# RWKV attention and a mixing MLP in one kernel: five hand-ordered engine queues replaced by a list scheduler's order

## The chip, the cores and the metric

The kernel runs on one core of one Trainium2 chip. Time is device microseconds of one execution, from the launch of the program to its end. Three runs of the kernel before took 586.89, 587.65 and 588.23 us, so the median is 587.65 us.

## The reference, cut to what matters

```python
# attention: 4 batches, 8 heads, 768 steps, head width 48, all fp32
for t in range(S):
    cur = einsum('bhd,bhe->bhde', u * k_t, v_t)
    y[:, :, t] = einsum('bhd,bhde->bhe', r_t, state + cur)
    state = w * state + einsum('bhd,bhe->bhde', k_t, v_t)
# the heads side by side are x [4, 768, 384]; then, for each batch
h = x.transpose(0, 2, 1) @ U @ V               # mixes the 768 steps, rank 32
u = x + h.transpose(0, 2, 1)
out = u + max(u @ w_ch1, 0) @ w_ch2            # 384 -> 1536 -> 384
```

The four weights `U`, `V`, `w_ch1` and `w_ch2` arrive as float64. The kernel reads them as pairs of 32-bit words and builds the fp32 value with integer operations.

## The kernel before, in words

**Attention.** The sequence of a batch is cut into 6 chunks of 128 steps, each of two halves of 64. Powers of `w` in tables (`tabT`, `tab`, `tabr`) turn the decay inside a chunk into plain products. Chunk n goes through preparation, two parts and an end.
- *Preparation.* `a_tr_r` and `a_tr_k` (lines 381 to 389) turn r and k so that the head width lies on the partitions, and scale them by `tabT`. Batch 0 does the turn with TensorE; batches 1 to 3 load r and k a second time as blocks of 32 by 32 (`a_load_blocks`, line 303, 32 DMAs for three chunks) and turn them on VectorE (line 369), with the product on GpSimd (line 371). `a_ks` (line 324) and `a_dv` (lines 331 to 334) are products on GpSimd; `a_dg` is a sum on VectorE, followed by 8 small multiplications on ScalarE (line 345), or in batch 0 by one product on VectorE (line 342).
- *Parts.* `a_part(n, 0)` and `a_part(n, 1)` issue some 60 small matmuls each: the output of chunk n and, between them, the scores and the state update of chunk n + 1. VectorE then masks the scores (`am`, line 557) and adds the state (`S`, line 581). The decayed state is made right behind that sum: one product on VectorE in batch 0 (line 583), four small multiplications on ScalarE in the others (line 585). The next part needs it.
- *End.* `a_x` (line 566) writes x. When all six chunks of a batch are there, `c_g` and `c_u` (lines 591 to 615) do the rank-32 mix. For batches 1 to 3 u is stored to HBM (`c_store`, line 669), read back as blocks (`c_blocks`, line 677) and turned on VectorE (`c_turn`, lines 689 to 691).

**MLP.** Each batch is two blocks of 384 steps with 12 hidden slices of 128. `m_1` makes one slice with 9 matmuls of 128x128 by 128x384, ScalarE its rounded high part `hh` (line 708), VectorE the remainder `hl` (line 709), and `m_2` (line 713) adds the slice to three outputs, again with 9 matmuls: 432 in a batch. `m_1` of the next slice stands between the two. The last slice adds u (line 726) and stores the output (line 728). The w_ch1 and w_ch2 matrices come as 24 units: DMA (line 174), conversion on ScalarE and VectorE (lines 182 to 191), the high half on ScalarE (line 201), the low half on GpSimd (line 202).

**Order.** Batch 0's attention is the front, and no MLP can run beside it. The attention of batch b + 1 is spread over the MLP of batch b at positions written by hand (`attn_slots`, line 753: loads at t0 - 9, preparation and parts at fixed steps). TensorE and SyncE, the engine that issues nearly all DMAs, follow that written order from the first MLP on; VectorE, ScalarE and GpSimd follow it from the MLP of batch 1 on, and before that an order that the framework works out. Each engine takes its queue strictly in turn, so an instruction whose data is not there holds all behind it. `wake` (line 76) adds matmuls without use to the front.

Of the kernel before, what the change touches and what calls it, by code (L numbers as in the profile page):

```python
# [19 lines left out]
W_HI = 1.0  # L20


@with_exitstack
def rwkv_moe(ctx: ExitStack, tc: tile.TileContext, r, k, v, w, u, U, V, w1, w2, out):
# [21 lines left out]
    NVS = 3  # L46
# [4 lines left out]
    ps = ctx.enter_context(tc.tile_pool(name="ps", bufs=1, space=bass.MemoryType.PSUM))  # L51

    def ps_tile(tag, name, bufs):
        return ps.tile([128, 512], F32, tag=tag, name=name, bufs=bufs)
# [5 lines left out]
    ident = const.tile([128, 128], F32, name="ident")  # L60
    make_identity(nc, ident)
    mask = const.tile([128, C2], F32, name="mask")
    nc.gpsimd.memset(mask, 1.0)
    for g in range(2):
        nc.gpsimd.affine_select(out=mask[g * C2:(g + 1) * C2], in_=mask[g * C2:(g + 1) * C2], pattern=[[1, C2]],
                                compare_op=ALU.is_gt, fill=0.0, base=0, channel_multiplier=-1)
# [7 lines left out]
    nc.scalar.copy(first_act, ident[0:1, 0:1])  # L74

    def wake(n):

        pt = ps_tile("mm", "p_wake", 2)
        for _ in range(n):
            nc.tensor.matmul(pt[:, :128], lhsT=ident, rhs=ident, start=True, stop=True)  # L80

    wT = const.tile([PD, NP, 1], F32, name="wT")
    nc.sync.dma_start(wT[:HP, :, 0], bass.AP(tensor=w.tensor, offset=w.offset, ap=[[1, HP], [2 * D, NP]]))
    nc.sync.dma_start(wT[HP:, :, 0], bass.AP(tensor=w.tensor, offset=w.offset + D, ap=[[1, D], [2 * D, NP]]))
    ub = const.tile([128, H, D], F32, name="ub")

    def tables():

        HC = C2 // 2
        NS = HC.bit_length()  # L90
        wc = const.tile([PD, NP, 1], F32, name="wc")
        nc.vector.tensor_scalar(wc, wT, W_LO, W_HI, ALU.max, ALU.min)
        sq = const.tile([PD, 2, NP, NS], F32, name="sq")
        pw = work.tile([PD, 2, NP, HC], F32, name="pw", tag="am", bufs=4)
        nc.gpsimd.memset(pw[:, :, :, 0:1], 1.0)
        nc.vector.tensor_copy(sq[:, 0, :, 0:1], wc)
        for i in range(1, NS):
            nc.vector.tensor_mul(sq[:, 0, :, i:i + 1], sq[:, 0, :, i - 1:i], sq[:, 0, :, i - 1:i])
        nc.vector.reciprocal(sq[:, 1], sq[:, 0])
        for i in range(NS - 1):  # L100
            m = 2 ** i
            for x_ in range(2):
                nc.vector.tensor_mul(pw[:, x_, :, m:2 * m], pw[:, x_, :, 0:m],
                                     sq[:, x_, :, i:i + 1].broadcast_to([PD, NP, m]))
        top = [sq[:, x_, :, NS - 1:] for x_ in range(2)]
        nc.vector.tensor_mul(tabT[:, 0, :, :HC], pw[:, 0], top[1].broadcast_to([PD, NP, HC]))
        nc.scalar.copy(tabT[:, 0, :, HC:C2], pw[:, 0])
        nc.vector.tensor_mul(tabT[:, 1, :, :HC - 1], pw[:, 1, :, 0:HC - 1],
                             pw[:, 0, :, HC - 1:].broadcast_to([PD, NP, HC - 1]))
        nc.scalar.copy(tabT[:, 1, :, HC - 1:2 * HC - 1], pw[:, 1])  # L110
        nc.gpsimd.tensor_copy(tabT[:, 1, :, C2 - 1:C2], top[1])
        for x_ in range(2):
            nc.scalar.copy(tabT[:, x_, :, C2:], tabT[:, x_, :, :C2])
        for x_, t in ((1, tab), (0, tabr)):
            pt = ps_tile("tr", f"pt_tab{x_}", 1)
            for q in range(NP):
                nc.tensor.transpose(pt[:, q * PE_:q * PE_ + PD], tabT[:, x_, q, :], ident[:PD, :PD])
            nc.scalar.copy(t.rearrange("p (h d) -> p h d", d=D), pt.rearrange("p (h d) -> p h d", d=HP)[:, :, :D])
        nc.vector.tensor_mul(wm, top[0], top[0])

    def flags():

        wrow = work.tile([1, DM], F32, name="wrow", tag="xh", bufs=NXS)
        nc.sync.dma_start(wrow, w.rearrange("(o h) d -> o (h d)", o=1))
        wrc = work.tile([1, DM], F32, name="wrc", tag="xh", bufs=NXS)
        nc.vector.tensor_scalar(wrc, wrow, W_LO, W_HI, ALU.max, ALU.min)
        nc.vector.tensor_tensor(wrc, wrc, wrow, ALU.not_equal)
        outside = const.tile([1, 1], F32, name="outside")
        nc.vector.tensor_reduce(outside, wrc, AX.X, ALU.max)
        nc.vector.tensor_copy(flag, outside)  # L130

    flag = const.tile([1, 1], I32, name="flag")
    tabT = const.tile([PD, 2, NP, C], F32, name="tabT")
    wm = const.tile([PD, NP, 1], F32, name="wm")
    tab = const.tile([128, DM], F32, name="tab")
    tabr = work.tile([128, DM], F32, name="tabr", tag="xl", bufs=NXS)
# [3 lines left out]

    NBIG = 30
# [4 lines left out]
    def big(shape, dt, name):  # L146
        return xpool.tile(shape, dt, tag="big", name=name, bufs=NBIG)

    Uf = const.tile([128, NCH, R], F32, name="Uf")
    V3 = const.tile([3 * R, S], F32R, name="V3")  # L150
# [6 lines left out]
    turn = [False]  # L157

    def unit(name, shape, parts, split):

        P_ = shape[0]
        n = 1
        for s_ in shape[1:]:
            n *= s_
        got = []

        def view(ap, two=1):
            return ap if len(shape) == 2 else ap.rearrange("p (a c) -> p a c", a=shape[1])

        def load():  # L170
            t = big([128, 2 * n], I32, f"raw_{name}") if wide else big([128, n], F32, f"raw_{name}")
            got.append(t[:P_])
            for p0, ap in parts:
                nc.sync.dma_start(view(t[p0:p0 + ap.shape[0]]), ap.bitcast(I32) if wide else ap)

        def convert():
            v_ = got.pop()
            if wide:
                word = v_.rearrange("p (n two) -> p two n", two=2)
                low, high = word[:, 0], word[:, 1]  # L180
                byte = v_.bitcast(U8).rearrange("p (n e) -> p n e", e=8)[:, :, 3]
                nc.scalar.activation(high.bitcast(F32), high.bitcast(F32), AF.Copy, scale=2.0 ** -112)
                if turn[0]:

                    nc.scalar.activation(low.bitcast(F32), byte, AF.Relu, scale=-2.0 ** -5, bias=c_top[:P_])
                    nc.scalar.activation(low, low.bitcast(F32), AF.Copy, scale=-1.0, bias=C_TOP)
                else:
                    nc.vector.tensor_scalar(low, byte, 2.0 ** -5, 7.0, ALU.mult, ALU.min)
                turn[0] = not turn[0]
                nc.vector.scalar_tensor_tensor(low, high, 3, low, ALU.logical_shift_left, ALU.bitwise_or)  # L190
                nc.vector.scalar_tensor_tensor(low, high, -2 ** 31, low, ALU.bitwise_and, ALU.bitwise_or)
                v_ = low.bitcast(F32)
            split(view(v_))
        return load, convert

    def weight_units():
        units = []

        def split(hi, lo):
            def go(sv):  # L200
                nc.scalar.copy(hi, sv)  # L201
                nc.gpsimd.tensor_tensor(lo, sv, f32(hi), ALU.subtract)
            return go

        def split_to(d, key, name):
            def go(sv):
                t = big([128, 2, DM], F32R, name)
                d[key] = t
                split(t[:, 0], t[:, 1])(sv)
            return go  # L210

        def u_split(sv):
            nc.scalar.copy(Uf, sv)

        def v_split(sl):
            def go(sv):
                nc.scalar.copy(V3[:, sl], sv)
                nc.vector.tensor_tensor(V3[2 * R:, sl], sv[2 * R:], f32(V3[2 * R:, sl]), ALU.subtract)
            return go

        units.append(unit("u", [128, NCH, R], [(0, U.rearrange("(c p) r -> p c r", p=128))], u_split))
        for j in range(S // DM):
            sl = slice(j * DM, (j + 1) * DM)
            units.append(unit(f"v_{j}", [3 * R, DM], [(i * R, V[:, sl]) for i in range(3)], v_split(sl)))
# [12 lines left out]
    loaded = {}  # L237
    wide_r = {}
    wide_k = {}
    pre = {}  # L240
    trs = {}
    scs = {}
    xs = {}
    St = {}


    def on_dve(n):
        return n >= NCH

    def a_load(n):  # L250
        b, c = divmod(n, NCH)
        ts = []
        if n < 4:
            t3 = xpool.tile([128, 2 * H * HP + DM], F32, tag="uTl" if n % 2 else "uTh", name=f"ld_{n}", bufs=2)
            rk = t3[:, :2 * H * HP].rearrange("p (i h d) -> p i h d", i=2, h=H)
            ts = [rk[:, 0], rk[:, 1], t3[:, 2 * H * HP:].rearrange("p (h d) -> p h d", h=H)]
            for i, (t, src) in enumerate(zip(ts, (r, k, v))):
                q = nc.scalar if n < 3 and i == 1 else nc.sync
# [282 lines left out]
    def a_done(n, row):  # L541
# [4 lines left out]
        if row == 0:  # L546
            return
# [440 lines left out]
```

## Time and profile before

| | |
|---|---|
| median of three runs | 587.65 us |
| profiled execution, its own time | 588.04 us |
| its span, first to last instruction | 586.2 us |
| TensorE matmul busy | 450.8 us (77%), 5023 matmuls |
| VectorE busy | 241.6 us (41%) |
| ScalarE busy | 180.5 us (31%) |
| GpSimd busy | 173.5 us (30%) |
| mean granted TensorE clock | 0.856 of full speed |

One execution is profiled. Busy time of an engine is the time in which at least one of its instructions runs; idle time counts against the kernel only where that engine, or one that waits for it, sets the end. The granted clock is given as a share of 2.4 GHz: 1.00 is that level and 0.50 is 1.2 GHz. SPq is the instruction queue of SyncE.

### The profile page before, as it was taken

The page shows a single profiled execution, that of the slowest core. Times are in us where ns is not written, and L with a number is a line of the kernel's source. Part 1 is how long each engine was busy: PE and PEld are TensorE (multiplying, and loading weights), DVE is VectorE, ACT ScalarE, POOL GpSimd, SP SyncE. Part 2 cuts the span into 40 slices and gives each one's busy share as a digit, 9 for nine tenths or more (in the row PEclk, how much of TensorE's full clock was granted, in tenths as well). Part 3 has the DMA queues.
Part 4 walks back from the last instruction along what each step waited for, and adds up shares of the span by engine and source line. Part 5 has one row for each costly group of instructions (what it writes and reads, how often), then busy time and mean ns, then how long its engine had stood idle before and what let it go on. Part 6 is the DMA issues. An engine that isn't in the chain of part 4 may idle for free.

```text
span 586.2 us, 12398 instructions
## 1 busy us (share of the span) xinstructions
PE 450.8 (77%) x5023; PEld 417.9 (71%) x5023; DVE 241.6 (41%) x516; ACT 180.5 (31%) x536; POOL 173.5 (30%) x168
## 2 busy tenths in 40 slices
PE   6647778356869996718958999707949999899994
PEld 6546668245758995718857998707948899799994
DVE  6657438948652424122425424213414523322211
ACT  2351127355542521105414422104324522221110
POOL 4633204756435101025433301007505500220000
PEclk8567659759888998859979999858898999999998
DMA  9999002972266005965563004866265102600101
GB/s 153 180 316 349 4 13 62 136 115 33 49 121 97 3 1 135 159 97 91 79 103 82 6 3 104 168 97 110 49 85 92 43 2 60 142 2 1 40 1 45
DMA packets 210833, 50.23 MB, mean 86 GB/s; under 512 B 201617, under 2 KB 207506, under 8 KB 210770
## 3 DMA queue, kind: packets, MB, share of 16 engines
q1 hardware_dynamic: 206018, 48.50, 42.4%
q10 hardware_dynamic: 4752, 0.89, 1.1%
q8 instruction: 41, 0.67, 0.5%
q14 instruction: 22, 0.18, 0.1%
HBM read 40.50 MB, written 8.85 MB: 84 GB/s over the span
## 4 chain that ended last, share of the span: by engine, by line
PE 33%; SPq 15%; DVE 4%; DMA 4%; POOL 4%; ACT 3%; issue 3%; DVEq 0%; POOLq 0%; ACTq 0%
PE p L480 27%; SPq L303 10%; SPq L677 2%; PE pav L434 2%; DMA ub<-ud 2%; ACT dv L345 2%; PE pav L440 1%; SPq L285 1%; DMA ud<-x 1%; SPq L273 1%; POOL rT L371 1%; POOL dv L331 1%; DMA bl<-in_r_dram 1%; DVE x L726 1%; DVE x L615 1%
## 5 line engine op out<-in xcount | busy, mean ns | idle before, releaser
L480 PE MATMUL p<-uTh,w1s 128*128 128x384 f32 x570 | 171.9, 356 | 27.8 <-ACT w1s L201 16.1
L480 PE MATMUL p<-w2s,hh 128*128 128x384 f32 x564 | 152.0, 349 | 0.0
L480 PE MATMUL p<-w2s,hl 128*128 128x384 f32 x288 | 101.0, 351 | 47.9 <-DVE hl L709 47.9
L480 PEld LDWEIGHTS p<-uTh,w1s 128*128 128x128 f32 x570 | 110.8, 200 | 34.6 <-ACT w1s L201 17.0
L709 DVE SCALAR_TENSOR_TENSOR hl<-p,hh 128x384 fp32r<-128x384 f32 x96 | 53.0, 553 | 174.9 <-ACT hh L708 174.8
L480 PEld LDWEIGHTS p<-w2s,hh 128*128 128x128 f32 x564 | 106.8, 198 | 1.1
L480 PE MATMUL p<-uTl,w1s 128*128 128x384 f32 x288 | 102.5, 356 | 3.8 <-POOL uTl L691 3.8
L708 ACT ACTIVATE hh<-p 128x384 fp32r<-128x384 f32 x96 | 46.8, 487 | 151.2 <-PE p L480 150.9
L480 PEld LDWEIGHTS p<-w2s,hl 128*128 128x128 f32 x288 | 57.0, 198 | 49.5 <-DVE hl L709 49.5
L480 PEld LDWEIGHTS p<-uTl,w1s 128*128 128x128 f32 x288 | 57.7, 200 | 7.4 <-POOL uTl L691 6.7
L691 POOL TENSOR_TENSOR uTl<-ut,uTh 128x384 fp32r<-128x384 f32 x21 | 21.7, 1033 | 134.0 <-ACT uTh L690 133.9
L345 ACT ACTIVATE dv<-ldv,dg 128x48 f32<-128x48 f32 x144 | 34.3, 322 | 74.3 <-DVE dg L340 69.8
L400 PE MATMUL pab<-rT,kT 48*64 48x64 f32 x768 | 35.6, 246 | 23.2 <-DVE S L581 16.5
L371 POOL TENSOR_TENSOR kT<-kT,tabT 112x512 f32<-112x512 f32 x18 | 23.2, 1296 | 94.5 <-DVE kT L369 90.3
L400 PEld LDWEIGHTS pab<-rT,kT 48*64 48x64 f32 x768 | 29.1, 154 | 25.4 <-issue 16.0
L585 ACT ACTIVATE S<-S,wm 112x48 f32<-112x48 f32 x120 | 30.3, 323 | 51.3 <-DVE S L581 51.2
L434 PE MATMUL pav<-vsw,am 64*64 64x48 f32 x384 | 37.4, 246 | 2.7 <-ACT seen L503 2.7
L440 PE MATMUL pav<-S,rT 48*64 48x48 f32 x704 | 37.7, 239 | 0.0
L434 PEld LDWEIGHTS pav<-vsw,am 64*64 64x64 f32 x384 | 31.0, 157 | 7.6 <-ACT seen L503 4.2
L440 PEld LDWEIGHTS pav<-S,rT 48*64 48x64 f32 x704 | 33.7, 157 | 0.2 <-issue 0.2
L434 PE MATMUL pav<-ldv,am 64*64 64x48 f32 x320 | 30.8, 239 | 3.9 <-DVE x L566 2.8
L371 POOL TENSOR_TENSOR rT<-rT,tabT 112x512 f32<-112x512 f32 x18 | 23.4, 1306 | 32.7 <-DVE rT L369 32.7
(122 smaller groups left out, 582.7 us busy)
## 6 DMA issues: line engine op xcount, KB each, us to landing
raw_w<-in_moe_w_ch_dram SPq DMA_DIRECT2D x24, 384.0 KB, 7.9
out_dram<-x SPq DMA_DIRECT2D x24, 192.0 KB, 2.4
bl<-in_k_dram SPq DMA_DIRECT2D x95, 48.0 KB, 2.5
bl<-in_r_dram SPq DMA_DIRECT2D x95, 48.0 KB, 2.4
ud<-x SPq DMA_DIRECT2D x21, 192.0 KB, 2.0
ub<-ud SPq DMA_DIRECT2D x84, 48.0 KB, 2.3
ldr<-in_r_dram SPq DMA_DIRECT2D x20, 192.0 KB, 3.6
ldk<-in_k_dram SPq DMA_DIRECT2D x20, 192.0 KB, 4.1
```

Of the source, the lines that this page charges most:

```text
L303: nc.sync.dma_start(t[32 * g:32 * g + 32, q, :, :ln], sv)
L345: nc.scalar.activation(dv[:, h], vt[:, h], AF.Copy, scale=dg[:, h:h + 1])
L371: nc.gpsimd.tensor_mul(xT[:PD], xT[:PD], tabT[:, i])
L400: return [lambda q=q, i=i: nc.tensor.matmul(pt[(i ^ j) * C2:(i ^ j) * C2 + C2, q * C2:(q + 1) * C2], lhsT=kT[rows, q, i * C2:(i + 1) * C2] ...
L434: return nc.tensor.matmul(to(q, j, i), lhsT=am[j][half, q, :], rhs=vsw[n][half, q, :] if j else vt[half, 2 * q, :], start=(row == 0 and q ...
L440: return nc.tensor.matmul(to(q, row, i), lhsT=rT[rows, q, i * C2:(i + 1) * C2], rhs=St[n, i][rows, q, :], start=False, stop=(row == 1 and ...
L480: last_mm[:] = [nc.tensor.matmul(*args, **kw)]
L585: nc.scalar.activation(sn[:, q], sn[:, q], AF.Copy, scale=wm[:, q])
L677: nc.sync.dma_start(bt[32 * g:32 * g + 32], rows[:, :, c0:c0 + 32])
L691: nc.gpsimd.tensor_tensor(ul[:, ct, :], ut, f32(uh[:, ct, :]), ALU.subtract)
L708: i_hh = nc.scalar.activation(hh, pt, AF.Relu)
L709: i_hl = nc.vector.scalar_tensor_tensor(hl, pt, 0.0, f32(hh), ALU.max, ALU.subtract)
```

## The change

All work of the fast path is first recorded as operations, each with its engine, a duration in ns, the buffers that it reads and writes, and a key. `Plan.schedule` then plays all five engines forward: of the operations that are ready it takes the one that can start first (at equal starts the one with the smaller key), moves that engine's clock on, lets DMAs land after a modelled time, and gives buffers of a ring out in their order of use. The instructions of all five engines are issued in the order of the starts that this gives, from the first one on. The steps written by hand become keys only.

```diff
+    AFTER = {"DVE": 33, "ACT": 33, "PE": 54, "POOL": 79, "SP": 28}
+    ISSUE = 42
+    LANDS = 1650
+    ...
+                now = min(t for t, _, _ in at)
+                for t, o, i in sorted((a for a in at if a[0] <= now + 1), key=lambda a: a[1].key):
+                    done = t + o.ways[i][1]
+                    if any(j != i and max(free[w[0]], self.ready_on(o, w[0]), lock if w[3] else 0) + w[1] < done - 1
+                           for j, w in enumerate(o.ways)):
+                        continue
+    ...
+    def run(self):
+        self.schedule()
+        for o in sorted(self.ops, key=lambda o: (o.start, o.n)):
+            o.fn()
+def dve(n):
+    return 130 + 1.09 * n
+def act(n):
+    return 285 + 0.6 * n
+def pool(n):
+    return 180 + 2.15 * n
```

Operations marked with `lock` are never planned at the same time on VectorE and GpSimd. Two-operand steps with both operands in SBUF get two ways, and the scheduler takes the one that ends first; this covers `a_ks`, both products of `a_dv`, the product with `tabT`, the low halves of the weights and of u, and the decayed state. The multiplication by `dg` may go to ScalarE (8 small ones) or to VectorE (one), and one step of the weight conversion to VectorE or ScalarE.

```diff
+    def on_either(n, fn, w_, r_, dk=0.0):
+        return op("POOL", pool(n), lambda: fn(nc.gpsimd), w_, r_, lock=True, dk=dk,
+                  alt=[("DVE", dve(n), lambda: fn(nc.vector), True)])
```

The state is kept undecayed. The sum that the chain waits for is one VectorE operation whose second operand was multiplied by the decay earlier, beside the matmuls; the table `tab` is scaled to match, and `tabr` and its two products in batch 0 are gone.

```diff
-                nc.vector.tensor_tensor(sn, ptv, St[n, i], ALU.add)
-                if plain(n):
-                    nc.vector.tensor_mul(sn, sn, wm.broadcast_to([PD, NP, D]))
-                for q in range(0 if plain(n) else NP):
-                    nc.scalar.activation(sn[:, q], sn[:, q], AF.Copy, scale=wm[:, q])
+                on_dve(192, lambda e, new=new, ptv=ptv, dec=decayed[n, j]: e.tensor_tensor(new.t, ptv(), dec.t, ALU.add),
+                       [new], [pt, decayed[n, j]])
+            dec = decayed[nk] = wbuf([PD, NP, D], F32, "SW", 2, f"SW_{nk[0]}_{nk[1]}")
+            on_either(192, lambda e, dec=dec, new=new: e.tensor_mul(dec.t, new.t, wm.t.broadcast_to([PD, NP, D])),
+                      [dec], [new, wm])
```

`m_2` issues the six matmuls with `hh` first and the three with `hl` last. All `wake` calls are gone. The blocks of r and k get a ring of 5 buffers of their own, and the pool that they shared with the weights goes from 30 to 25.

```diff
-            whole(pt, lhsT=hh[:, ts_], rhs=W2[f][:, 0], start=(f == 0), stop=False)
-            whole(pt, lhsT=hh[:, ts_], rhs=W2[f][:, 1], start=False, stop=False)
-            whole(pt, lhsT=hl[:, ts_], rhs=W2[f][:, 0], start=False, stop=(f == NFT - 1))
+        for part, m, h in ((high, 2, hh), (low, 1, hl)):
+            for i in range(TPB):
+                n = b * NCH + t * TPB + i
+                pe(m * MM, lambda part=part, i=i: part(i), [ops[n]], [h, W2[f]])
```

The keys, in us, place the loads and the attention of the next batch earlier against the MLP than the slots before did:

```diff
+    T0, PER = 46.0, 1.95
+    FRONT, EACH = 9.0, 5.5
+    begin = [T0 + 49 * PER * b for b in range(B)]
+    ...
+            t0, per = ((begin[b - 1] + 34, 8.0), (begin[b - 1] + 8, 11.0))[b > 1]
+            for c in range(NCH):
+                at(t0 + per * c - per - 16, lambda n=n0 + c: a_load(n))
+            for c in range(0, NCH, 3):
+                for i in (1, 3, 0, 2):
+                    at(t0 + per * c - per - 18 + 0.1 * i, lambda n=n0 + c, i=i: (a_load_blocks(n, i, 0), a_load_blocks(n, i, 1)))
+    with tc.manual_schedule(engines={mybir.EngineType.PE, mybir.EngineType.SP, mybir.EngineType.DVE,
+                                     mybir.EngineType.Activation, mybir.EngineType.Pool}):
+        plan.run()
```

## Rows read from the trace of the kernel before

**Rows 1.** Stage table: window, its length, busy us (instructions) of each engine, clock, DMA.
```profile
core 0: us, PE busy (x) PEld busy (x) DVE busy (x) ACT busy (x) POOL busy (x), PEclk, DMA share, GB/s
0.00:84.30 84.30, 55.70 (x920) 50.12 (x921) 46.45 (x114) 23.20 (x56) 30.37 (x38) 0.66 0.72 174
84.30:226.50 142.20, 110.67 (x1228) 100.58 (x1227) 83.73 (x156) 64.66 (x187) 58.74 (x52) 0.85 0.41 69
226.50:368.40 141.90, 107.37 (x1229) 97.88 (x1229) 48.98 (x112) 40.43 (x135) 42.04 (x39) 0.88 0.48 86
368.40:504.40 136.00, 103.15 (x1223) 95.75 (x1223) 44.63 (x103) 38.89 (x132) 39.29 (x37) 0.89 0.46 82
504.40:578.90 74.50, 73.92 (x425) 73.60 (x425) 17.82 (x33) 13.35 (x27) 3.07 (x3) 1.00 0.10 24
```

**Rows 2.** The same table, of the MLP's matmuls alone, one batch.
```profile
368.40:504.40 136.00, 86.21 (x433) 0.89 0.46 82
```

**Rows 3.** SyncE's queue in time, second boundary of batches: start, duration, DMAs in a run.
```profile
242.10 8.28 SPq L303 DMA_DIRECT2D bl<-in_k_dram  x16
250.43 8.15 SPq L303 DMA_DIRECT2D bl<-in_r_dram  x16
```

**Rows 4.** VectorE's queue in time there: what ended its idle time stands in brackets.
```profile
239.89 0.56 DVE L709 SCALAR_TENSOR_TENSOR hl<-p,hh 128x384 fp32r<-128x384 f32 x1 [2.32 <-ACT hh L708]
260.68 0.45 DVE L369 STREAM_TRANSPOSE rT<-bl 128x256 f32<-128x256 f32 x1 [3.90 <-DMA ub<-ud]
261.05 0.98 DVE L709 SCALAR_TENSOR_TENSOR hl<-p,hh 128x384 fp32r<-128x384 f32 x2
```

**Rows 5.** Waits of SyncE's queue from 84.3 to 368: us in total, times, longest.
```profile
SPq L669 <- DVE x L615: 107.3, 5, 33.7
```

**Rows 6.** TensorE's longest waits, one each of 84.3:226.5, 226.5:368.4 and 368.4:504.4.
```profile
PE p L480 <- ACT w1s L201: 16.1, 3, 13.9
...
PE p L480 <- DVE hl L709: 22.0, 2, 15.6
...
PE p L480 <- DVE hl L709: 25.6, 2, 17.5
```

**Rows 7.** The front on VectorE: ends of chunks 0, 2, 3 and 5 (x).
```profile
29.59 0.56 DVE L566 TENSOR_TENSOR x<-pav,dv 128x384 f32<-128x384 f32 x1 [0.40 <-PE pav L440]
53.50 0.56 DVE L566 TENSOR_TENSOR x<-pav,dv 128x384 f32<-128x384 f32 x1 [3.19 <-PE pav L440]
59.02 0.55 DVE L566 TENSOR_TENSOR x<-pav,dv 128x384 f32<-128x384 f32 x1
79.37 0.56 DVE L566 TENSOR_TENSOR x<-pav,dv 128x384 f32<-128x384 f32 x1 [8.97 <-PE pav L440]
```

**Rows 8.** The front on TensorE: first of two runs of matmuls without use.
```profile
70.36 2.93 PE L80 MATMUL p_wake<-ident 128*128 128x128 f32 x12
```

**Rows 9.** The front on VectorE between chunks 0 and 1: a wait in the queue.
```profile
39.57 0.55 DVE L218 TENSOR_TENSOR V<-raw_v,V 32x384 fp32r<-32x384 f32 x1 [4.25 <-ACT V L217]
```

**Rows 10.** Groups by line: busy us, mean ns of one, idle before.
```profile
L190 DVE SCALAR_TENSOR_TENSOR raw_w<-raw_w 128x384 int32<-128x384 int32 x24 | 21.2, 894 | 0.6 <-ACT raw_w L186 0.2
L191 DVE SCALAR_TENSOR_TENSOR raw_w<-raw_w 128x384 int32<-128x384 int32 x24 | 19.0, 804 | 0.3
L583 DVE TENSOR_TENSOR S<-S,wm 112x192 f32<-112x192 f32 x10 | 5.4, 537 | 0.0
L342 DVE TENSOR_TENSOR dv<-ld,dg 128x384 f32<-128x384 f32 x4 | 3.3, 836 | 0.1
L331 POOL TENSOR_TENSOR dv<-ldr,ldk 128x384 f32<-128x384 f32 x20 | 20.7, 1037 | 24.5 <-DVE x L566 17.5 <-issue 4.2 <-ACT S L585 2.7
```

**Rows 11.** One line: shortest, median and longest ns of one.
```profile
L191 DVE SCALAR_TENSOR_TENSOR raw_w<-raw_w x24: 543/556/1436, 46.9 to 156.6; 128x384 int32<-128x384 int32 x24
```

**Rows 12.** TensorE in time: pairs of MLP matmuls behind a pause, and in the last batch.
```profile
231.94 1.01 PE L480 MATMUL p<-uTh,w1s 128*128 128x384 f32 x2
504.66 0.51 PE L480 MATMUL p<-uTh,w1s 128*128 128x384 f32 x2
```

More of the change, by code (lines that the diff above doesn't have):

```diff
@@ L176, in convert, with join @@
+        def join():
+            nc.vector.scalar_tensor_tensor(word(0), word(1), 3, word(0), ALU.logical_shift_left, ALU.bitwise_or)
+            nc.vector.scalar_tensor_tensor(word(0), word(1), -2 ** 31, word(0), ALU.bitwise_and, ALU.bitwise_or)
         def convert():
-            v_ = got.pop()
             if wide:
[L179 to L192, printed above, removed]
@@ L347, in a_pre @@
[L347 to L365 removed]
+        kt, kb = ks_[n]
@@ new lines, in reads, with a_first, a_part, first @@
+    def reads(n, j, i):
+        return [*trs[n], kss[n], *vs[n][1]]
+    seen = {}
+    def a_first(n):
+        abs_[n] = [bank(t, f"pab_{n}_{j}") for j, t in enumerate(AB)]
+        a, b_ = p_sc(n, 0) + p_su(n, 0), p_sc(n, 1) + p_su(n, 1)
+        pe(1000, lambda: in_turn(a, b_), abs_[n], reads(n, 0, 0), tiled=True)
+        ams[n] = [None, None]
+        for j in range(2):
+            a_am(n, j)
+        for i in range(2):
+            a_st(n, i)
+    def a_part(n, row):
+        nxt = (n + 1) % NCH
+        last = n % NCH == NCH - 1
+        if row == 0:
+            if nxt:
+                abs_[n + 1] = [bank(t, f"pab_{n + 1}_{j}") for j, t in enumerate(AB)]
+            avp[n] = bank("mm" if front(n) and n % 2 else "av", f"pav_{n}")
+        o = 1 - row
+        mine = p_out(n, row)
+        other = p_sc(n + 1, o) + p_su(n + 1, o) if nxt else []
+        def first():
+            in_turn(mine, other)
+            opened.append(n)
+        def second():
+            if opened:
+                whole(avp[n].t[:, DM:DM + 1], lhsT=ident_, rhs=ident_[:, :1], start=False, stop=False, skip_group_check=True)
+            i = mine[0]()
@@ new lines, in second, with see @@
+            in_turn(mine[1:], other[1:])
+        rd = [*ams[n], vsw[n], *vs[n][1], trs[n][0]] + [St[n, i] for i in range(2) if (n, i) in St]
+        wr = [avp[n]]
+        if nxt:
+            rd += reads(n + 1, o, o)
+            wr += [abs_[n + 1][o]]
+        t = None
+        if row == 0:
+            pe(600 if last else 1000, first, wr, rd, tiled=True)
+            t = wbuf([128, 1], F32, "seen", 2, f"seen_{n}")
+            def see():
+                seen[n] = nc.scalar.copy(t.t[C2:C2 + 1], avp[n].t[C2:C2 + 1, 7 * D - 1:7 * D])
+            op("ACT", 150, see, [t], [avp[n]])
+            seens[n] = t
@@ new lines, in attention @@
+    def attention(b, t0, per, lead, step):
+        n0 = b * NCH
+        for c in range(NCH):
+            n = n0 + c
+            t = t0 + per * c
+            prepare(n, t - per - lead if c else t - 2 * lead)
+            if c == 0:
+                at(t - 1, lambda n=n: a_first(n))
+            at(t, lambda n=n: a_part(n, 0))
+            at(t + per / 2, lambda n=n: a_part(n, 1))
+            at(t - 0.1, lambda n=n: a_dg(n))
+        return t0 + per * NCH
+    end = attention(0, FRONT, EACH, 1.0, 0)
```

1038 lines of the change are left out of this document (540 added, 498 removed).

## The prediction

> **What bounds the kernel now.** The stage table comes first [rows 1]. It is cut at the first MLP matmul of each batch's own stretch: the front ends at 84.3 us, then come batches 0, 1, 2 and 3 with 142.2, 141.9, 136.0 and 74.5 us, and 586.2 - 578.9 = 7.3 us of last store. Batch 3 does the same MLP as the others, and its stretch is all TensorE: 73.92 of 74.5 us busy at a clock of 1.00. So 74.5 us is what a batch's MLP takes when nothing holds it. Batches 0 to 2 carry the attention of the next batch as well. In batch 2 the MLP's matmuls hold 86.21 of TensorE's 103.15 busy us [rows 1, 2], so everything else it does there is 103.15 - 86.21 = 16.9 us. A batch at full clock without a wait would take 74.5 + 16.9 = 91.4 us, against 136 to 142. Batches 1 and 2 thus lose 50.5 and 44.6 us, of which 34.5 and 32.9 us are idle TensorE and the rest is low clock; batch 0 loses 50.8. No other engine explains that: VectorE is busy 49 of 142 us in batch 1, GpSimd 42.
>
> The waits tell what holds TensorE. In batches 1 and 2 its longest is on `hl`, 22.0 and 25.6 us in two waits each [rows 6]. A step of 0.56 us cannot itself cost 17 us, so the queue ahead of it has to be read [rows 4]: `hl` is made at 239.89, the next only at 261.05, and between them VectorE sits in front of the block transposes of the next attention, the last of them until 260.68. Those wait for their blocks, and SyncE's queue shows why they are late [rows 3]: 32 block loads are issued one after the other from 242.10 to 258.58, at the moment when they are wanted. SyncE could have done that much earlier; from 84.3 to 368 it stood 107.3 us in five waits, 33.7 the longest, in front of a store of u whose data was not there [rows 5], with the loads behind it. This is head-of-line blocking in two queues, once per batch boundary.
>
> Batch 0 is different: TensorE's longest wait is for weights (16.1 us on the high halves, 13.9 of it at once [rows 6]), while VectorE is busy 83.7 us and ScalarE 64.7 [rows 1]. The front is a chain: chunks end at 29.59, 53.50, 59.02 and 79.37 [rows 7], so a chunk takes between 5.5 us (2 to 3) and an average of 10.2 (3 to 5).
>
> **The change part by part.** *Loads and queue order, batches 1 and 2.* No work is removed; SyncE issues in the order in which data is planned to be ready, so a store of u no longer stands ahead of loads, and `hl` goes ahead of transposes whose blocks are planned to land later. The keys put a chunk's loads 24 to 29 us ahead of its first part (its step plus 16 or 18), where now they are issued at the boundary. That removes the long `hl` waits, and with them most of the low clock behind them. What is late next are short waits: an order fixed in advance stalls wherever a real instruction is longer than planned. I put 5 us on each batch, which is a fifth of the `hl` wait that goes: 91.4 + 5 = 96.4 us. The bounds are 91.4 (all gone) and 115 (half of the loss stays). `m_2` with `hl` last gives `hl` six matmuls more cover, about 1.0 us at the last batch's rate (74.5 us over 432 is 0.172 each), and costs nothing.
>
> *The decay beside the chain.* VectorE's decay product (537 ns, ten in batch 0 [rows 10]) leaves the chain between two parts; two per chunk are 1.1 us, 5.4 in all. The same number of products is still issued, on VectorE or GpSimd beside some 60 matmuls; if a part starts before its product is done, it costs the product again, 0.5 us. In batches 1 to 3 four small ScalarE steps go from behind the sum; TensorE's long waits there are on `hl` [rows 6], and I count nothing.
>
> *The front.* The `wake` matmuls in the chain go, two runs of 2.93 us in its last chunk [rows 8], 5.9 us. One queue stall on VectorE (4.25 us for a weight [rows 9]) goes too. Against that, without `wake` more of the front runs at the lower clock. By its own chain I take chunk 0 to end at 22 us (7.6 earlier than 29.59: part of the stretch behind the first loads is queueing), then 6.5 us for each of five chunks, between the undisturbed 5.5 and the average 10.2, near the former because the 10.2 contains the wake runs; then the 4.9 us from 79.37 to 84.3 as before: 22 + 32.5 + 4.9 = 59. The bounds: 20 + 27.5 + 4.9 = 52, and with 9.0 a chunk 22 + 45 + 4.9 = 72. A loss is excluded only as far as these rows go; a front that is as long as now costs 25 us more.
>
> *Batch 0 and the weights.* VectorE's work up to the end of batch 0 is 46.5 + 83.7 = 130 us [rows 1]. The two joining steps of the conversion average 894 and 804 ns over 24 weights [rows 10], while the second has a median of 556 [rows 11]; at 556 each they would be 26.7 instead of 40.2 us. So the work is 117 to 130 us, and front and batch 0 together can hardly be shorter than that. The forecast gives them 59 + 105 = 164 us, 71 to 79% of VectorE. Batch 0 at TensorE's pace is 91.4 plus about 1.7 for six more rank-32 products; with conversions started in the front's gaps I put 12 us of waiting for weights on it: 105, between 93 and 142 (nothing gained). Batch 3 stays at 75, the end at 7.3.
>
> *A step that moves from GpSimd to VectorE* takes 836 ns in the fourth row of [rows 10], a product of two operands, and has a median of 556 in another two-operand form [rows 11], for 1037 on GpSimd [rows 10]. I count nothing for it outside batch 0. [Rows 11] show one instruction between 543 and 1436 ns: VectorE is sometimes held. The Trainium skill, "SBUF — State Buffer", section "Who interferes with whom", says that VectorE instructions with two SBUF inputs and GpSimd instructions that read SBUF shut each other out for the whole instruction. The trace agrees with that spread. By that rule a moved step relieves the port only by being shorter, and the rival that follows would be the outcome; the sum stands without it.
>
> *The sum.* 59 + 105 + 96.4 + 96.4 + 75 + 7.3 = 439.1 us of span. The profiled execution took 588.04 for a span of 586.2, so 1.8 more: 441 us. That execution is 0.4 us above the median of the runs, which I neglect.
>
> **The rivals.**
> - *VectorE and GpSimd bind front and batch 0.* For it: VectorE's joins take up to three times their shortest in [rows 10, 11], and 117 to 130 us of VectorE plus 89 of GpSimd (30.4 + 58.7, [rows 1]) meet there. Against it: both are spread over 226 us now, with VectorE 42% idle. Price: front 72 (its upper bound), batch 0 130: 72 + 130 + 96.4 + 96.4 + 75 + 7.3 + 1.8 = 479 us.
> - *The planned order does not fit the chip.* All engines now keep one order from the first instruction, where front and batch 0 had another. For it: one VectorE form varies by 900 ns [rows 11]. Against it: the change plans this form with 130 + 1.09 x 384 = 549 ns, 1% off its median of 556, and a GpSimd product with 180 + 2.15 x 384 = 1006 for a measured 1037 [rows 10]. Half of the present loss stays in batches 1 and 2 (115 each), front 65, batch 0 115: 494 us.
> - *Buffers hold the loads.* The blocks get five buffers, four hold three chunks, so the second three chunks' loads wait for the third chunk. For it: 32 loads need 16.4 us [rows 3]. Price: 16.4 and some 6 for landing, turning and products, 23 us in each of three batches: 441 + 69 = 510. Against it: the attention has slack inside a batch, and the MLP can go on.
> - *Slower: a clock that stays down.* Behind a pause a pair of MLP matmuls takes 1.01 us instead of 0.51 [rows 12]; in the front the clock is 0.66 on average [rows 1]. If many short waits keep the granted clock at the lower of its levels, 1.2 GHz, through whole MLPs, each batch costs 74.5 us more; two are 441 + 149 = 590 us. It decides from two whole batches on. Against it: the batches now recover to 0.85 to 0.89 despite waits of 17 us. The Trainium skill, "TensorE: Matmul & The Clock Gate", section "What's actually happening", calls the lower clock the default that activity releases, which fits both rows.
> - *It does nothing.* If the waits come from the work and not from the order, the time stays near 588. Against it: [rows 3 to 5].
>
> **How the numbers follow.** Forecast 0.57, VectorE and GpSimd 0.18, misfit of the order 0.11, buffers 0.07, clock 0.04, nothing 0.03. Faster by over 0.2% (about what a measurement of this kernel can tell from no change) is 0.57 + 0.18 + 0.11 + 0.07 = 0.93; of the last two, 0.02 are no change and 0.05 slower. The forecast's own range is 410 (front 52, batch 0 at 93, batches 1 and 2 at 91.4: 52 + 93 + 183 + 75 + 7.3 + 1.8 = 412, and 2 for an earlier first chunk) to 465 (front 65, batch 0 115, the others 100). The range reaches through the first two rivals and takes in 505, leaving out the rest and the tails.
>
> **What would show it.** Right: one stretch of TensorE at a clock near 1.00 from the first MLP on, no wait on `hl` above 3 us, block loads in SyncE's queue spread over a batch and long before their transposes, front near 59, stages near 96. Wrong in the front: chunks 9 us apart at a clock near 0.6. Wrong in batch 0: TensorE waits for weights of over 20 us. The order is wrong if VectorE or ScalarE stand idle in front of one instruction while `hl` or `hh`, ready, is behind it. The forecast fails as a whole if batches 1 and 2 stay above 115 us.

## The result: 466.5 us, and the profile after

The changed kernel takes 466.49 us (median of four runs, 463.31 to 467.75) against 587.27 (585.91 to 588.23) for the kernel before on the same chip: a ratio of 0.7937, 95% interval 0.7893 to 0.798. 441 us was forecast, with a range of 410 to 505. One run of the experiment e4 below, at 470.4 us, fell in a slower state of the chip and is not in its ratio; every other number is of fast runs. The profiled execution took 466.91 us for a span of 465.2. From its page, first the busy time of each engine with share and instructions:

```profile
PE 418.7 (90%) x4967; PEld 392.8 (84%) x4967; DVE 295.7 (64%) x670; ACT 131.4 (28%) x301; POOL 43.5 (9%) x51
```

GpSimd has lost 130 of its 173.5 us, VectorE has gained 54. Then the same span in 40 equal slices, busy share in tenths:

```profile
PE   3778869779989798799999999999999999999992
DVE  5977689999999475788377756566752454113111
POOL 2321001320111100200010000111100000000000
PEclk9755558999999998899999999999999999999998
```

From slice 18 on TensorE is full, at or near full clock. What is left lies ahead of that: a low clock in slices 3 to 6, then, in slices 7 to 13, VectorE at nine tenths. The stage table of after answers to [rows 1]. A stage ends, as the last three do there, where a batch's own MLP ends. (The prediction calls these points the next batch's first MLP matmul; for batch 1 of before that matmul is at 230.37 and not at 226.5, so the rest of its attention and its rank-32 mix count to its own stretch. The same holds here, with 193.70.) The last row is the end:

```profile
core 0: us, PE busy (x) PEld busy (x) DVE busy (x) ACT busy (x) POOL busy (x), PEclk, DMA share, GB/s
0.00:70.30 70.30, 49.46 (x865) 42.44 (x866) 52.41 (x139) 41.58 (x100) 12.36 (x21) 0.63 0.95 208
70.30:185.80 115.50, 102.02 (x1226) 93.94 (x1224) 98.97 (x213) 40.41 (x91) 15.14 (x15) 0.96 0.66 128
185.80:287.90 102.10, 98.55 (x1234) 93.06 (x1232) 70.43 (x161) 18.84 (x44) 6.44 (x6) 0.98 0.65 120
287.90:382.00 94.10, 93.67 (x1216) 88.70 (x1216) 53.47 (x122) 17.43 (x41) 9.55 (x9) 1.00 0.32 68
382.00:456.70 74.70, 74.70 (x433) 74.64 (x431) 19.02 (x37) 13.14 (x27) 0.00 (x0) 1.00 0.07 21
456.70:465.20 8.50, 0.26 (x2) 0.00 (x0) 1.44 (x3) 0.00 (x0) 0.00 (x0) 0.80 0.22 76
```

| stage | before | forecast | after | off by |
|---|---|---|---|---|
| front | 84.3 | 59 | 70.3 | +11.3 |
| batch 0 | 142.2 | 105 | 115.5 | +10.5 |
| batch 1 | 141.9 | 96.4 | 102.1 | +5.7 |
| batch 2 | 136.0 | 96.4 | 94.1 | -2.3 |
| batch 3 | 74.5 | 75 | 74.7 | -0.3 |
| end | 7.3 | 7.3 | 8.5 | +1.2 |

The misses add to 26 us, the difference between 441 and 466.9. 22 of them lie ahead of 185.8 us.

The long waits of batches 1 and 2 are gone. Of TensorE's waits (total, times, longest) over the whole kernel, these are the largest total and the only one on `hl`, which was 22.0 and 25.6 us in [rows 6]:

```profile
PE p L274 <- DVE w2s L460: 5.1, 3, 2.4
...
PE p L274 <- DVE hl L917: 0.4, 1, 0.4
```

SyncE's queue in time around the end of batch 0 (start, duration, DMAs in a run) shows why, against [rows 3]. The 32 block loads that were issued in one go when they were wanted are now spread over a batch, some of them ahead of the stores of u (L871) and between them:

```profile
95.81 4.91 SPq L550 DMA_DIRECT2D bl<-in_r_dram  x8
116.73 5.33 SPq L550 DMA_DIRECT2D bl<-in_k_dram  x8
...
178.45 2.46 SPq L550 DMA_DIRECT2D bl<-in_k_dram  x5
181.01 1.38 SPq L871 DMA_DIRECT2D ud<-x  x3
182.44 0.43 SPq L550 DMA_DIRECT2D bl<-in_k_dram  x1
```

SyncE still waits long, with [rows 5] its counterpart:

```profile
SPq L948 <- DVE x L947: 80.9, 5, 35.3
SPq L871 <- DVE x L825: 32.0, 4, 27.8
```

These waits now cost little: VectorE waits 5.1 us at the longest for a block, and TensorE not for `hl` but for the 0.4 us above.

### The profile page after: what moved, and what is told of

It reads as the page before. It is cut to its first block, busy times and chain, and to the rows that moved or that the text cites. A ratio compares the mean times of both kernels' runs of the same rounds, so it can differ in the third digit from the quotient of the medians.

```text
span 465.2 us, 11942 instructions
## 1 busy us (share of the span) xinstructions
PE 418.7 (90%) x4967; PEld 392.8 (84%) x4967; DVE 295.7 (64%) x670; ACT 131.4 (28%) x301; POOL 43.5 (9%) x51
## 4 chain that ended last, share of the span: by engine, by line
PE 61%; SPq 14%; DVE 12%; DMA 6%; issue 3%; ACT 2%; DVEq 0%; ACTq 0%
PE p L274 48%; SPq L881 4%; SPq L550 4%; PE pav L653 4%; PE pav L659 3%; SPq L522 3%; DMA ub<-ud 2%; PE pab L619 1%; DVE w2s L460 1%; PE pu L274 1%; SPq L529 1%; DMA ub<-in_u_dram 1%; DVE hl L917 1%; SPq L418 1%; PE pab L635 1%
## 5 line engine op out<-in xcount | busy, mean ns | idle before, releaser
L274 PE MATMUL p<-uTh,w1s 128*128 128x384 f32 x576 | 151.6, 344 | 1.3 <-DVE w1s L460 1.0
L274 PE MATMUL p<-w2s,hh 128*128 128x384 f32 x576 | 120.7, 341 | 7.5 <-DVE w2s L460 5.1
L274 PEld LDWEIGHTS p<-w2s,hh 128*128 128x128 f32 x576 | 99.9, 188 | 11.2 <-DVE w2s L460 6.0
L274 PEld LDWEIGHTS p<-uTh,w1s 128*128 128x128 f32 x576 | 105.8, 193 | 3.5 <-DVE w1s L460 1.3
L274 PE MATMUL p<-w2s,hl 128*128 128x384 f32 x288 | 67.8, 340 | 0.0
L619 PE MATMUL pab<-rT,kT 48*64 48x64 f32 x768 | 35.3, 248 | 2.8 <-DVE S L778 2.8
L653 PEld LDWEIGHTS pav<-ldv,am 64*64 64x64 f32 x320 | 23.4, 143 | 9.2 <-issue 7.3
L560 POOL TENSOR_TENSOR ks<-ldk,tab 128x384 f32<-128x384 f32 x14 | 14.8, 1063 | 129.2 <-PE pab L635 54.1
L635 PE MATMUL pab<-ldv,ks 64*48 64x48 f32 (+1 forms) x576 | 22.8, 221 | 0.0
L778 DVE TENSOR_TENSOR S<-pab,SW 112x192 f32<-112x192 f32 x40 | 13.8, 344 | 13.5 <-PE pab L635 8.5
L590 DVE STREAM_TRANSPOSE kT<-bl 128x256 f32<-128x256 f32 x36 | 15.3, 429 | 10.4 <-DMA bl<-in_k_dram 5.2
```

What stands on the lines that cost most here:

```text
L274: return nc.tensor.matmul(*args, **kw)
L560: on_either(384, lambda e: e.tensor_mul(ks.t, kt()[:, :, :D], by_head(tab.t)), [ks], kb + [tab])
L590: on_dve(256, lambda e, qh=qh, bl=bl: e.transpose(xT.t[:, 2 * qh:2 * qh + 2].rearrange("p q (m t) -> p q m t", m=4), bl.t[:, :, m0:m0 + 4, ...
L619: return [lambda q=q, i=i: nc.tensor.matmul(pt.t[(i ^ j) * C2:(i ^ j) * C2 + C2, q * C2:(q + 1) * C2], lhsT=kT.t[rows, q, i * C2:(i + 1) * ...
L635: return nc.tensor.matmul(pt.t[j * HP:j * HP + m, SU + q * D:SU + (q + 1) * D], lhsT=ks.t.rearrange("p h d -> p (h d)")[half, k0:k0 + m], ...
L653: return nc.tensor.matmul(to(q, j, i), lhsT=am[j].t[half, q, :], rhs=vsw[n].t[half, q, :] if j else vt()[half, 2 * q, :], start=(row == 0 ...
```

## The experiments

The first question is what brought the 121 us: the order, the planned times in it, the choice of engine, or the decay. The second is where the 22 us of front and batch 0 went. All ratios are against the kernel before; after has 0.7937 [0.7893, 0.798], and 0.01 is 5.9 us.

**e3: the kernel before, with only its loads moved.** For batches 2 and 3 the loads of the first two chunks and the first 32 of the 64 block loads are issued at step 36.5 of the 49 of an MLP, a quarter of it ahead of its end, where they stood before; all else is as before.

```diff
-        at(t0 - 9, lambda: (a_load(n0), a_load(n0 + 1)))
-        for i in (1, 3, 0, 2):
-            blocks(n0, i, t0 - 9)
+        if b == 1:
+            early_loads(b, at, t0 - 9)
+        if b + 1 < B:
+            early_loads(b + 1, at, 36.5)
```

> The kernel before, with one edit: the first two chunks' loads and the first blocks of batches 2 and 3 are issued at step 36.5 of 49 of the MLP before, instead of at its end. Theory (late loads are what the two long waits on hl come from): the waits of 15.6 and 17.5 us go, with a few us of low clock behind each, 587 to 545 (540 to 553). Rival (the queue order as a whole is the cause, and the next late instruction takes their place): less than 12 us gained, 575 or more.

Measured 547.8 us, ratio 0.9339 [0.9264, 0.9414]: 38 us, as the theory had it. TensorE's long waits on `hl`, 47.6 us in batches 1 and 2 of the kernel before, are down to this:

```profile
PE p L480 <- DVE hl L709: 13.8, 2, 7.3
```

The head-of-line blocking in [rows 3 to 5] is thus shown to be the cause of 34 of those 47.6 us, and moving these loads alone is worth a third of the gain.

**e7: the plan does not know that a DMA takes time to land.**

```diff
-    LANDS = 1650
+    LANDS = 0
...
-                queues = max(queues, t + ns) + o.dma
+                queues = t + ns
```

> The scheduler's kernel, planned as if every DMA's data were there when its issue ends; keys, buffers and engines' durations as they are. Theory (the order is good because the plan knows when data lands): instructions are put ahead of data that is not there, and head-of-line waits return at the boundaries and on block transposes: 480 to 530. Rival (issuing loads early is all that matters, and the landing times in the plan decide nothing): 464 to 472.

485.02 us, ratio 0.8255 [0.8226, 0.8284]: 18.5 us lost. Not where the expectation put it: the front ends at 92.2 us instead of 70.3, and batch 0's last three MLP matmuls start at 199.2 instead of 185.4, so 14 of the 18.5 us are lost by then. In the front ScalarE's queue has the first step of 17 weights nearly in a row, most of them waiting for their DMA (32.9 to 51.4 us), and small steps behind them that the others need: `seen`, a copy of one element, for TensorE, and the high part of V for VectorE. TensorE's longest wait in e7, then VectorE's waits on V and, at the boundaries of batches, on u read back from HBM:

```profile
PE pav L653 <- ACT seen L731: 19.4, 2, 10.1
```

```profile
DVE ut L891 <- DMA ub<-ud: 25.1, 10, 6.0
DVE V L470 <- ACT V L469: 11.4, 1, 11.4
```

In after, TensorE's wait in that row is 0.9 us, there is no wait on V among VectorE's, and the one on u is:

```profile
DVE ut L891 <- DMA ub<-ud: 10.8, 11, 1.8
```

**e10: the plan knows no durations** (500 ns for everything but DMAs).

```diff
-        o.ways = [(eng, ns, fn, lock)] + list(alt)
+        if not dma:
+            ns = 500
+        o.ways = [(eng, ns, fn, lock)] + [(a, 500, f, l) for a, _, f, l in alt]
```

> The scheduler's kernel, planned with 500 ns for every instruction group but the DMAs, whose issue and landing stay as they are. Theory (the plan's durations make the order good; a group of nine matmuls at 500 instead of 522 and a part at 500 instead of 1000 let TensorE run ahead in the plan): waits for hl and for weights return, 480 to 510. Rival (dependencies, keys and landing times give nearly the same order): 464 to 472.

498.34 us, ratio 0.8477 [0.8445, 0.8508]: 32 us lost, over the front (84.2) and all MLPs. TensorE now waits for small steps all over, `hl` and `hh` among them:

```profile
PE p L276 <- ACT hh L918: 12.9, 5, 4.1
PE pav L655 <- ACT seen L733: 8.8, 3, 4.4
...
PE p L276 <- DVE hl L919: 5.8, 4, 2.5
```

A list scheduler with wrong times still keeps 89 of the 121 us. The 32 us are not the price of the order alone: with 500 ns for either way, the plan also sends more steps to GpSimd, which is busy 125.0 us instead of 43.5, and the next two runs price such a choice at up to 9 us. An issue order straight from the keys, without the scheduler, was not tried.

**e1 and e9: no choice of engine.** All steps that may go to either engine on GpSimd (e1) or on VectorE (e9).

```diff
-        return op("POOL", pool(n), lambda: fn(nc.gpsimd), w_, r_, lock=True, dk=dk,
-                  alt=[("DVE", dve(n), lambda: fn(nc.vector), True)])
+        return op("POOL", pool(n), lambda: fn(nc.gpsimd), w_, r_, lock=True, dk=dk)    # e1
+        return op("DVE", dve(n), lambda: fn(nc.vector), w_, r_, lock=True, dk=dk)      # e9
```

> The scheduler's kernel, but each two-operand step that had two ways may go to GpSimd alone, as in the kernel before. In the changed kernel about 85 us of such steps run on VectorE; on GpSimd they last about 1.9 times as long, some 160 us more there. Theory (the choice of engine is worth something by itself, because a GpSimd product of 1.0 to 1.3 us stands in the attention's preparation): slower than the changed kernel by 8 to 25 us, 474 to 491. Rival (VectorE binds batch 0, 99 of 115 us busy, and the scheduler hands it too much): the same or up to 10 us faster, 456 to 467. If the choice were the main source of the 121 us, it would be above 520.

> The scheduler's kernel, with every step that may choose placed on VectorE; GpSimd then computes nothing behind the tables. In the kernel that chose, 36 of them ran on GpSimd, 28 us. Theory (the choice is worth what it saves in time for which the two engines shut each other out; one engine alone never waits for the other): within 5 us of 466.5, 462 to 471, and no VectorE instruction of the weights' joins above 0.7 us. Rival (VectorE is the bound of front and batch 0, so each step put on it is paid there, 36 x 0.55 = 20 us): 480 or more.

e1 took 474.3 us, 0.8091 [0.8034, 0.8148], and e9 473.71, 0.8076 [0.803, 0.8122]. The choice is worth some 8 to 9 us against either side. e9 came out between the two expectations, just above the theory's; as the theory said, no join of the weights took over 0.7 us (0.56 at most). The stage tables of e1 and of e9 (front, batch 0) show opposite ways to the same time:

```profile
0.00:94.00 94.00, 45.77 (x864) 39.84 (x865) 71.47 (x154) 48.40 (x107) 37.43 (x50) 0.64 0.87 191
94.00:189.80 95.80, 95.50 (x1226) 90.82 (x1225) 57.83 (x123) 27.08 (x61) 67.04 (x67) 0.99 0.64 122
```

```profile
0.00:74.90 74.90, 48.39 (x867) 41.07 (x868) 54.10 (x146) 40.61 (x88) 1.25 (x10) 0.68 0.88 191
74.90:189.90 115.00, 103.45 (x1225) 95.28 (x1226) 103.45 (x233) 38.61 (x88) 0.00 (x0) 0.94 0.65 128
```

In e1 batch 0 runs at TensorE's pace (95.5 of 95.8 us busy), but the front is 94 us long: from 57 to 72 us VectorE does one weight conversion after the other with the state sum `S` behind them, and TensorE is idle (`PE pab L618 <- DVE S L777`, 16.3 us the longest). In e9 VectorE is busy 103 of 115 us of batch 0.

**e6 and e5: GpSimd for some of these steps.** In e6 the low halves of the weights go to GpSimd, in e5 also those of u and the preparation of batches 1 to 3; all else is free.

```diff
-    def on_either(n, fn, w_, r_, dk=0.0):
+    def on_either(n, fn, w_, r_, dk=0.0, only=False):
...
-                  alt=[("DVE", dve(n), lambda: fn(nc.vector), True)])
+                  alt=[] if only else [("DVE", dve(n), lambda: fn(nc.vector), True)])
```

> The scheduler's kernel with GpSimd alone for the low halves of the 24 weights, 22 of which ran on VectorE (14.1 us). Theory (VectorE binds batch 0): 5 to 10 us faster than 466.5, 456 to 462. Rival (the low half is on the way to the MLP, and 1.0 instead of 0.55 us makes each weight later): 466 to 474.

> The scheduler's kernel with GpSimd alone for the low halves of the weights and of u and for the preparation products of batches 1 to 3; the attention of batch 0 and the decay keep their choice. With GpSimd alone everywhere the front took 94 us and batch 0 96; with the choice 70 and 115. Theory (in batch 0 VectorE binds, 99 of 115.5 us busy, and the choice overloads it): the front stays near 70, batch 0 falls to 97 to 105, 448 to 458 in all. Rival (front and batch 0 together are bound by conversions that must be done somewhere, and a shorter batch 0 was only a longer front): 463 to 475.

e6: 472.47 us, 0.8044 [0.8015, 0.8074]; e5: 476.58, 0.8093 [0.8057, 0.813]. My theory fell twice: the plan's own choice is better than both. What GpSimd takes over, VectorE pays for in part, as the two joins of the weight conversion show. They are the same 48 VectorE instructions in every kernel, and they sum to 40.2 us before, 28.1 after, 35.3 in e1, 40.3 in e5, 31.3 in e6 and 26.6 in e9, where GpSimd has next to nothing. (They do not grow in step with GpSimd's busy time: up to the end of batch 0 it is 104.5 us in e1 and 88.7 in e5.) The joins' rows in after (answering to the first two of [rows 10]), then in e5:

```profile
L440 DVE SCALAR_TENSOR_TENSOR raw_w<-raw_w 128x384 int32<-128x384 int32 x24 | 14.1, 589 | 0.8
...
L439 DVE SCALAR_TENSOR_TENSOR raw_w<-raw_w 128x384 int32<-128x384 int32 x24 | 14.0, 584 | 0.0
```

```profile
L439 DVE SCALAR_TENSOR_TENSOR raw_w<-raw_w 128x384 int32<-128x384 int32 x24 | 20.3, 846 | 0.0
L440 DVE SCALAR_TENSOR_TENSOR raw_w<-raw_w 128x384 int32<-128x384 int32 x24 | 20.0, 832 | 0.8
```

**e4: useless matmuls in the front.** Three of 128x128 behind each of batch 0's 12 parts (36 matmuls, 72 records in the trace), to see what the low clock costs.

```diff
+        def extra():
+            if front(n):
+                for _ in range(WAKE):
+                    whole(avp[n].t[:, DM:DM + 128], lhsT=ident_, rhs=ident_, start=False, stop=False, ...)
```

> The scheduler's kernel with three matmuls without use (128x128 by 128x128, into columns that nothing reads) behind each of batch 0's 12 parts, 36 in all. Theory (the front is paced by TensorE at the lower of its clock levels, 0.50 from 20 to 70 us): they raise the granted clock for part of the front, parts and turns take half as long there, the front ends near 58 to 64 instead of 70.3, and the time is 453 to 461. Rival (the clock stays down, or the front is paced by VectorE and the loads): 36 matmuls of 0.2 to 0.4 us are added to the chain, 472 to 482.

461.1 to 466.1 us, ratio 0.7893 [0.7817, 0.797]: not clearly different from after, so neither the gain nor the loss that was expected. The clock did rise. The same 10 us of the front in after and in e4 (the last three columns are clock, DMA share and GB/s):

```profile
40.00:50.00 10.00, 7.53 (x147) 6.39 (x140) 5.98 (x14) 8.79 (x19) 0.21 (x1) 0.50 1.06 376
```

```profile
40.00:50.00 10.00, 8.32 (x163) 7.52 (x164) 7.77 (x20) 9.79 (x21) 0.83 (x1) 0.87 1.06 375
```

The front ended at 66.6 instead of 70.3, and batch 0 took 115.1 us as before.

**e12: a plan for a slow front.** The parts of batch 0 are planned at twice their time.

```diff
-        pe(1000, lambda: in_turn(a, b_), abs_[n], reads(n, 0, 0), tiled=True)
+        pe(2000 if front(n) else 1000, lambda: in_turn(a, b_), abs_[n], reads(n, 0, 0), tiled=True)
```

> The scheduler's kernel, with batch 0's parts planned at 2000 ns instead of 1000 (the last chunk's at 1200 instead of 600), the length that they have at the clock of 0.50 that the trace shows from 20 to 70 us; nothing else. Theory (the front is longer than I put it because its order was made for parts of half their length): it ends at 60 to 66 instead of 70.3, 457 to 463. Rival (the chain through TensorE at the low clock takes that long in any order): 465 to 470.

466.95 us in five rounds, ratio 0.7949 [0.7913, 0.7986]: no change, as the rival had it. But its stages are quite other ones (front, batch 0):

```profile
0.00:88.00 88.00, 47.63 (x865) 41.05 (x866) 69.97 (x172) 57.58 (x125) 23.24 (x29) 0.63 0.95 209
88.00:185.00 97.00, 96.73 (x1226) 92.03 (x1224) 79.65 (x180) 20.13 (x47) 12.17 (x11) 0.98 0.62 114
```

A front of 88 us instead of 70.3 costs nothing: 17 of the 24 weights are joined in it, against 8 in after, and batch 0 then runs at TensorE's pace. Front and batch 0 trade time with each other: batch 0 ends between 179.9 and 190.3 us in after and in all its variants but e7 and e10, while the front ends anywhere from 66.6 to 94.0.

**e2: the decay back in the chain, e8: `m_2` in the old order, e11: five fillers and the old `m_2` together.**

```diff
-                on_dve(192, lambda e, ...: e.tensor_tensor(new.t, ptv(), dec.t, ALU.add), ...)
+                on_dve(192, lambda e, ...: e.tensor_tensor(new.t, ptv(), old.t, ALU.add), ...)      # e2
+            on_dve(192, lambda e, new=new: e.tensor_mul(new.t, new.t, wm.t.broadcast_to([PD, NP, D])), ...)
...
-                pe(m * MM, lambda part=part, i=i: part(i), [ops[n]], [h, W2[f]])
+            pe(3 * MM, lambda i=i: (high(i), low(i)), [ops[n]], [hh, hl, W2[f]])                   # e8
```

> The scheduler's kernel with the state's decay back in the chain: the sum, then the product by the decay, both on VectorE, and the next part waits for the second; the product beside the chain is gone. Theory: costs only in the front, where a part waits for the state, 11 steps of 0.35 to 0.5 us: 4 to 6 us, 470 to 473, and nothing beside the MLPs. Rival (the decay carries a large share of the gain): over 480. Rival (no part of the front waits for the state, it is paced by TensorE's own work at the low clock): within 2 us of 466.

> The scheduler's kernel with the second matmul stage in its order of before: hh, hh, hl for each output in turn, one operation that waits for hl at its start. Theory (one slice of the first stage, 1.55 us, covers hh and hl, 0.49 + 0.55 us, where ScalarE and VectorE come at once): 465 to 469. Rival (VectorE's queue makes hl late in batch 0, and hl last is what hides that): 474 to 490.

> The scheduler's kernel with five instead of three matmuls without use behind each of batch 0's parts, and the second matmul stage in its order of before. The filler of three raised the clock of the front and ended it 3.7 us earlier, the order of before ended the profiled execution 3.6 us earlier; neither was clear of 466.5 in time. If both are real and add up: 455 to 461. If the front is paced by VectorE's queue and the loads once the clock is up: 462 to 468.

e2: 467.49 us, 0.7963 [0.7916, 0.8009]. e8: 463.42 us, 0.7897 [0.7862, 0.7933]. e11: 465.76 us, 0.7937 [0.7898, 0.7976]. None can be told from after. The decay beside the chain and the order within `m_2` bring nothing that can be measured; for the decay that means 1.5 us, with an interval of 2.5 or more to either side of each time. e8's middle value lies 2.4 us below after's, but the intervals overlap and e11, which contains it, shows nothing. No version clearly beats the changed kernel. With the choice of engine worth 9 us at most, and the decay, the order within `m_2` and fillers in the front nothing that shows, the order in which things are issued is left, by elimination, for most of the 121 us. How that divides between the earlier keys, the scheduler and the blocks' own buffers was tested only as far as e3, e7 and e10 go.

## Why the prediction was right, and where it was off

The range was wide enough to take in two rivals, and 466.5 us is 25 from the forecast and 13 from the first rival's 479. So the total alone does not speak for the forecast; the stages do, in part.

**Batches 1 and 2: right.** 196.2 us together for a forecast of 192.8. They gained 82 us. e3 shows the part of the loads by itself, 38 us, and the head-of-line mechanism with it; the rest came with the order as a whole. Wrong durations lose some 12 us behind batch 0 (e10), wrong landing times some 5 (e7). Batch 1 is 5.7 longer for a reason that the forecast left out: batch 0 leaves some of batch 1's attention undone, so its first 9.2 us hold 6.31 us of TensorE work at a clock of 0.85, and its MLP starts at 193.7.

**Front plus batch 0: the mis-sized term.** Forecast 59 + 105 = 164 us, measured 185.8; that is 22 of the 26 us. The step that did not hold is "the work is 117 to 130 us"; the bound that it gave for the two stages was too low to show that 164 us is tight. The joins did fall, from 40.2 to 28.1 us. But VectorE's work up to the end of batch 0 rose to 52.4 + 99.0 = 151.4 us, since GpSimd's fell from 89.1 to 27.5 [rows 1]: about 33 us of other work came to VectorE (151.4 - 130.2 + 12.1). "I count nothing for it outside batch 0" said where it would matter, and then the sum had nothing inside batch 0 either. The table of after for a stretch inside batch 0 and for 80 to 150 us shows what it makes:

```profile
100.00:110.00 10.00, 8.68 (x47) 8.19 (x48) 9.90 (x21) 3.59 (x7) 0.50 (x1) 1.00 0.13 19
...
80.00:150.00 70.00, 61.38 (x874) 55.49 (x873) 68.63 (x148) 24.45 (x52) 12.63 (x12) 1.00 0.61 113
```

VectorE is busy 68.6 of 70 us, and TensorE has 8.6 us of gaps in them. In all of batch 0 the gaps are 13.5 us, of which 6.7 are waits for weights; the forecast had 12 for these. This is the first rival's mechanism, at 185.8 between the forecast's 164 and its 202; of its two engines VectorE is the full one, with GpSimd 27.5 of 185.8 us busy. The runs bear it out for batch 0: with 80 us of VectorE or less in it (e1 57.8, e12 79.7) it runs at TensorE's pace, 95.8 and 97.0 us, near the lower bound of 93; with 89 to 103 us (after, e2, e4, e5, e6, e8, e9) it takes 110 to 118. Whoever cleared VectorE's work out of batch 0 paid about as much in the front.

That VectorE's sum sets the end of batch 0 is not shown. In e1 it is 71.5 + 57.8 = 129.3 us, within the prediction's own 117 to 130, and batch 0 still ends at 189.8: the plan put the conversions in a row ahead of the front's chain, and GpSimd had 104.5 us. In after VectorE is idle for 18 of the 70.3 us of the front. A plan that does conversions in those gaps was not tried, so what holds the two stages near 185 us together stays open.

**The front as a term of its own** was 11.3 us too short: chunk ends 25.51, 34.86, 43.22, 52.09, 58.43 and 63.34 (+0.55) for a forecast of 22 and then 6.5 each. Its clock was 0.50 from 20 to 70 us, which the text named as the price of taking `wake` out. The first three steps from chunk to chunk, of 9.4, 8.4 and 8.9 us, are the sign that the prediction gave for a wrong front. But e4 and e12 show that the front's length is not what the total hangs on. The share of the low clock in it stays open: the fillers that lift the clock take TensorE's time themselves (18.3 us of busy time in e11), so the two can't be parted with them.

**The decay: 5.4 us that did not show.** e2 puts the product back and loses nothing measurable. It was in the chain of the front, and e12 shows a front that grows without a loss.

**`m_2` "costs nothing": right** (e8). Its cover was counted wrong: two matmuls with `hh` stood ahead of the first `hl` before, so six are four more, 0.7 us, and not six. It is hardly needed either: TensorE waits 0.4 us for `hl` in after and 1.2 in e8, with the old order.

**The other rivals.** "The planned order does not fit" was right to fear wrong times (e7, e10), but with the change's own times the waits of batches 1 and 2 stay short. Buffers: no wait for loads of 16 us or more appears; the longest for a block is 5.1. The clock does not stay down through an MLP: 0.98 and 1.00 in batches 1 and 2.

## What to carry to other kernels

Before an engine is made the place for moved work, add that work to its busy time in the stage where it is already the fullest, and ask which stage will do it. Two stages that pass work to each other should be forecast as one term: here a front of 66.6 or of 88 us gave the same total. When queues are in order, a wrong position of a load can cost more than most of what one tunes in the instructions (38 us here for moving loads alone), and a plan with wrong durations or landing times gave back 32 and 18.5 us of the gain.

## What the runs showed of the hardware

A row of GpSimd products kept VectorE out for all of them. In e1, VectorE's queue in time, then GpSimd's:

```profile
73.74 6.25 DVE L438 SCALAR_TENSOR_TENSOR raw_w<-raw_w 128x384 int32<-128x384 int32 x1
80.02 0.56 DVE L439 SCALAR_TENSOR_TENSOR raw_w<-raw_w 128x384 int32<-128x384 int32 x1
```

```profile
73.68 1.99 POOL L459 TENSOR_TENSOR w2s<-raw_w,w2s 128x384 fp32r<-128x384 f32 x2
75.63 2.96 POOL L459 TENSOR_TENSOR w1s<-raw_w,w1s 128x384 fp32r<-128x384 f32 x3
78.55 1.02 POOL L459 TENSOR_TENSOR w2s<-raw_w,w2s 128x384 fp32r<-128x384 f32 x1
```

A join whose median in that run is 0.55 us took 6.25: it began 0.06 us after the first of six products and ended 0.4 us after the last. The Trainium skill, "SBUF — State Buffer", section "Who interferes with whom", has the one that is second blocked for the whole instruction; here it was blocked for six. So a step handed to GpSimd can cost VectorE its full GpSimd duration (about 1.0 us for 128x384) instead of its 0.55 us on VectorE. In e9, where GpSimd computes next to nothing, the longest of the 48 joins took 0.56 us. The plan marks the joins and these products with `lock`, in e1 too, so it never puts them side by side. Once the real times have shifted, they meet all the same. In after, with GpSimd busy for 43.5 us in all, the longest join took 1.38 us.

The clock did not rise in the front of after, with TensorE busy 6.8 to 9.0 of every 10 us from 20 to 70 in small matmuls (48x64 and the like): granted 0.50, which is 1.2 GHz, in each of these stretches. In e4, with 72 records of full 128x128 matmuls between them, it was 1.00, 0.66, 0.87 and 0.96 in the four stretches from 20 to 60. The Trainium skill, "TensorE: Matmul & The Clock Gate", section "What's actually happening", has the gate follow how busy the engine has been. The profile's busy time does not show that here: 8.95 of 10 us busy at 0.50 (after, 20 to 30) against 7.04 at 1.00 (e4), with 180 and 178 matmul records. Busy time is itself longer at the lower clock, so it does not compare the two. The edit shows that the fillers raise the clock; what about them does it was not tested.
